# One plan for all eight PSUM banks, attention scores in rounds of 256 columns, another order in the first norm, and a fourth home for q, k and v

## The chip, the cores and the metric

The kernel runs on one core of a Trainium2 chip. The time is that of the device in microseconds (us), the median of several executions. Lower is better. TensorE is called PE here, VectorE DVE, ScalarE ACT, GpSimd POOL and SyncE SP; PEld is the loading of weights into the PE array.

## What is computed

The input `x` has 2048 rows of 512 in bf16. Four layers are applied to it, attention A, feed-forward B, A, B, each on a normalised `x` and added back to it:

```
x = x + A(layernorm(x));  x = x + B(layernorm(x));  x = x + A(layernorm(x));  x = x + B(layernorm(x))

A: 32 heads of 16, the 2048 rows in 4 segments of 512
   logits = q_s k_s^T * 16**-0.5, causal inside the segment;  a_dot = softmax(logits) v_s
   a_mem  = phi(q_s) M / (phi(q_s) z + 1e-6);   o = g a_mem + (1-g) a_dot
   M += phi(k_s)^T v_s;  z += sum phi(k_s);     phi(t) = t+1 if t > 0 else exp(t);   result o wo
B: gelu(x w_gate) * (x w_up) w_down, 512 -> 1792 -> 512
```

## The kernel before

**Work.** The rows are handled as 8 passes `k` (4 segments in each of the two attention layers), every pass with an `Att(k)` and an `Ffn(k)`. Weights stay in SBUF. A dense product is one PSUM bank (128 partitions x 512 columns of fp32): 4 matmuls of 512 columns for q, k, v, wo, gate and up, 14 for down. In a pass these are 4 blocks each of q and k, 4 row tiles of v, 4 of wo, 14 tiles of gate, 14 of up and 4 row tiles of down.

**Scores.** Heads come in 4 blocks `b` and 2 parities `par`, four heads at a time, each head in its own 32 rows of the PE array (row tiles; line 794). With odd heads `kB`, a copy of `kf` with the even heads masked out, takes the place of `kf`. Causal scores of one head against 512 queries are four pieces of 512, 384, 256 and 128 columns, by key tile `ki`. Five steps (`PAIRS`) of four heads x 512 columns serve two parities, so a pass has 20 steps. A step fills four banks `st`, in two halves of two heads; ACT takes the exponential of each half (line 828, 128x1024), POOL zeroes what lies above the diagonal (line 817). When the planner finds only the first half's banks free, it issues the step as two separate halves (`score_now`, `score`). When a parity is complete, a "flush" multiplies `pt` with `vaug` (v with a column for the sum) in column tiles of 32 into a dense bank (line 847), and DVE divides and transposes it back (lines 859 to 874).

**Modes of PE.** A matmul uses the whole 128x128 array (line 370, `whole`), four column tiles of 32 (line 367, `columns`, used for dense products near a flush) or four row tiles (`rows`, scores). The planner keeps `ck.mode` and charges 0.097 us for a change of it.

**The order of work** is written out by a planner inside the kernel: the engines run in manual order, and `order()` keeps clocks of PE, ACT, DVE, POOL and SP and issues an instruction when its clock says that it is due. Dense products, memory products and flushes are `Item`s with a due time; free PSUM banks and `pt` buffers are counted in `banks`, `st_free` and `step_free`; numbers in `POLICY` shift the due times. Where nothing is ready while scores are still to come, a product of ones (`warm`) fills the gap. The order on each engine is therefore fixed in the program: a late operand stalls the whole engine.

**Banks.** Four banks (`M_BANKS`, tiles `m0` to `m3`) belong to dense products and flushes, four to scores (`st0` and `st1`, two banks each).

**The start.** Tiles of `x` for the first segment arrive by four DMAs, two issued by SP and two by ACT (line 248), the gate vector `beta` behind them on ACT's queue, and then SP issues wk, wq, the second segment of x, wv and the third segment of x (line 239). PE runs 16 `warm` products. The norm of the first segment is written by hand: DVE computes the statistics of tiles 0 to 2 (lines 1044, 1047), ACT those of tile 3 (lines 1061, 1062, stored in `shift` and `mv`) behind two small exponentials of `beta` (lines 300, 302); a small DVE addition (line 1050) and POOL's power (line 1054) give the scales of tiles 0 and 1 and then of 2 and 3; then DVE writes the four normalised tiles (line 426), PE transposes them (line 468) and the first k and q follow (lines 744, 749).

**The end.** In the second layer the row tiles of down are added to `x` by DVE (line 914) and written out by SP (line 239) one by one.

Of the kernel before, what the change touches and what calls it, by code (L numbers as in the profile page):

```python
# [34 lines left out]
WARM = 16  # L35
PAIRS = 5
STEPS = 4 * PAIRS
BY_PE = {("xnTf", 0), ("xnTf", 1), ("xnTf", NK - 1)}
M_BANKS = 4
PT_STEPS = 5  # L40
# [5 lines left out]
SPLIT = 8  # L46
# [4 lines left out]
    flush_wait=5.276, piece_slack=1.333, kb_slack=3.5, mem_slack=1.0, margin=1.079, qk_due=0.75, e_q=0.099,  # L51
    e_k=0.898, exp_slack=-1.27, e_slack=2.265, phi_slack=3.273, gelu_slack=-1.15, act_evict=0.538,
    first_evict=0.928, gate_step=0.002, up_due=1.3, up_step=0.02, down_due=1.6, down_step=0.042, upd_due=0.5,
    v0_due=-0.54, x1_at=11.9, x2_at=22.0, cut_slack=0.0, direct=1, gelu_tiles=3, kb_dve=1, phi_pool=2,
    half_steps=1)
# [54 lines left out]
class Clocks:  # L110
# [6 lines left out]
    def __init__(self):  # L117
        self.pe = 0.0
        self.mode = "whole"
        self.act, self.dve, self.pool, self.sp = Engine(0.09), Engine(0.07), Engine(), Engine()  # L120
        self.engines = (self.dve, self.act, self.pool, self.sp)
        self.later, self.seq, self.waiting = [], 0, []
        self.dma = 0.0
        self.ev = {}
# [47 lines left out]
    def has(self, *names, by=None):  # L172
        t = self.pe if by is None else by
        return all(self.ev.get(n, 1e9) <= t for n in names)
# [24 lines left out]
class Item:  # L199


    def __init__(self, due, ready, ops, done, kind, ps):
        self.due, self.ready, self.ops, self.done, self.kind, self.ps = due, ready, ops, done, kind, ps
        self.posted = 0.0
# [17 lines left out]
def order(pol, nc, cst, seg, wrk, psp, st_pool, A_x, A_wq, A_wk, A_wv, A_wo, A_beta, B_x, B_w_gate, B_w_up, B_w_down, out):  # L222

    ck = Clocks()
    ev = ck.ev
    xf = A_x.flatten_outer_dims()
# [8 lines left out]
    wd_sb = cst.tile([P, FT, D], BF16, name="wd_sb")  # L235
    beta_bc = cst.tile([P, H], BF16, name="beta_bc")
# [21 lines left out]
    for n, (sb, w) in enumerate(((wg_sb, B_w_gate), (wu_sb, B_w_up))):  # L258
        for kt in range(KT):
            for h in range(2):  # L260
                c = slice(FF * h // 2, FF * (h + 1) // 2)
                pieces.append((37.0 + 1.6 * (8 * n + 2 * kt + h), 224, lambda sb=sb, w=w, kt=kt, c=c: load(
                    sb[:, kt, c], w_view(w)[:, kt, c])))
    for h in range(7):
        r = slice(2 * h, 2 * h + 2)
        pieces.append((94.0 + 2.0 * h, 256, lambda r=r: load(
# [7 lines left out]
    def bank_tile(i, shape, dtype=F32):  # L274
        return psp.tile(shape, dtype, tag=f"m{i}", bufs=1, name="m")

    def keep_warm(n, bank):
        if n:
            ps = bank_tile(bank, [P, L])
        for _ in range(n):  # L280
            nc.tensor.matmul(ps[:], lhsT=warm[:], rhs=wide, start=True, stop=True)
# [18 lines left out]
    nc.scalar.activation(out=tmp_e[:], in_=beta_bc[:], func=ACT.Exp)  # L300
    tmp_e2 = cst.tile([P, H], F32, name="tmp_e2")
    nc.scalar.activation(out=tmp_e2[:], in_=beta_bc[:], func=ACT.Exp, scale=-1.0)
# [3 lines left out]
    vaugs = [cst.tile([P, TPS, VW + 15], BF16, name=f"vaug{i}") for i in range(SETS)]  # L306
# [10 lines left out]
    def later_constants():  # L317
# [4 lines left out]
        for n, va in enumerate(vaugs):  # L322
            ck.dve.post(13.0 + 3.0 * n, NORMAL, (0.4, lambda va=va: column(va), None))
# [10 lines left out]
    banks = [0.0] * M_BANKS  # L334

    class Psum:
        def __init__(self, shape=(P, L), dtype=F32):
            self.shape, self.dtype, self.bank, self.t = list(shape), dtype, None, None

        def __call__(self):  # L340
            if self.t is None:
                self.t = bank_tile(self.bank, self.shape, self.dtype)
            return self.t
# [4 lines left out]
    def evict(ps, dst, src, told, slack=NORMAL):  # L348
# [7 lines left out]
        first = pol.first_evict if ("scores", pol.half_steps - 1) not in ev and pol.half_steps else pol.act_evict  # L356
# [26 lines left out]
    class Norm:  # L383
# [80 lines left out]
        def first_turn(self, j):  # L464
            xn = self.first_xn[j]
            ps = bank_tile((j + 1) % M_BANKS, [P, KT, P], BF16)
# [3 lines left out]
            if j < 2:  # L470
                nc.scalar.activation(out=dst, in_=ps[:], func=ACT.Copy)
            else:
                nc.vector.tensor_copy(out=dst, in_=ps[:])
# [7 lines left out]
    class Att:  # L481
        def __init__(self, k):
            self.k, self.s, self.tt0 = k, k % NSEG, TPS * (k % NSEG)
            self.norm = Norm(("xnTa", k), self.tt0, f"xnTa{k % 2}", NORMAL, lambda: k < 2 or ("qkv", k - 2) in ev)
            self.vaug = vaugs[k % SETS]
# [8 lines left out]
        def add_items(self):  # L494
            k, s = self.k, self.s

            def storage():
                return k < SETS or (("scores", k - SETS) in ev and self.phi_done(k - SETS))
# [8 lines left out]
            def qk(b, w, done):  # L507
                ps = Psum()
                pairs = [(lambda kt=kt: w[:, kt, b * P:(b + 1) * P], lambda kt=kt: self.norm.xnT[:, kt, :])
                         for kt in range(KT)]  # L510
                return Item(k - pol.qk_due + 0.01 * b, lambda: storage() and ck.has(("xnTa", k)), dense(ps, pairs),
                            lambda: (made(), self.counted(), done(b, ps)), kind="qk", ps=ps)
# [30 lines left out]
            def v(j):  # L543
# [4 lines left out]
                def done():  # L548
# [6 lines left out]
                            lambda: ck.has(("xnTa", k)) and (k < SETS or ("flush", k - SETS, 3, 1) in ev),  # L555
                            dense(ps, pairs), done, kind="v", ps=ps)
# [61 lines left out]
        def mem_items(self):  # L618
# [5 lines left out]
            den = Psum((P, TPS, 4, 8))  # L624

            def den_mm(j, b):
                nc.tensor.matmul(den()[:, j, b, :], lhsT=self.phiq[:, b, j * P:(j + 1) * P],
                                 rhs=mem_state[k - 1][1][:, b, :], start=True, stop=True)

            def den_done():  # L630
                def add():
# [3 lines left out]
                        out=self.rdm[:], in0=den()[:], scalar=EPS_MEM, op0=ALU.add, op1=ALU.mult,  # L635
# [8 lines left out]
                              den_done, kind="mem", ps=den))  # L644

            def num(b):
# [32 lines left out]
                def go():  # L679
# [5 lines left out]
                            kind="mem", ps=ps)  # L685
# [4 lines left out]
        def upd_item(self):  # L690
            k = self.k
            psm = Psum((P, 4, P))
# [6 lines left out]
            def m(c):  # L699
                j, b = divmod(c, 4)  # L700
                nc.tensor.matmul(psm()[:, b, :], lhsT=self.phik[:, j, b * P:(b + 1) * P],  # L701
                                 rhs=by_head(self.vaug)[:, j, 8 * b:8 * b + 8, 0:DH], start=(c == 0), stop=(c == n_mm - 1))

            def done():
# [7 lines left out]
                def gated(src):  # L712
                    return lambda: nc.vector.tensor_tensor(out=made[0][:], in0=src()[:],
# [10 lines left out]
                if self.s == 0:  # L724
                    steps = [(0.154, lambda: nc.vector.tensor_copy(out=zacc[:], in_=self.zk[:]), kept),
                             (0.683, gated(psm), None),
                             (0.2, z, told),
                             (0.683, lambda: nc.vector.tensor_copy(out=macc[:], in_=psm()[:]), psm.read)]
                else:
                    steps = [(0.683, lambda: nc.vector.tensor_tensor(out=macc[:], in0=macc[:], in1=psm()[:],  # L730
# [3 lines left out]
                             (0.683, gated(lambda: macc), None),  # L734
# [4 lines left out]
                              done, kind="upd", ps=psm))  # L739
# [13 lines left out]
        def score_ready(self, t):  # L753
            b, i = divmod(t, PAIRS)
            if self.k == t == 0:
                return ck.has(("q", 0, 0), by=ck.pe - 0.055)
            names = [("q", self.k, b), ("k", self.k, b)] + ([("kB", self.k, b)] if i > 1 else [])
            return ck.has(*names, by=ck.pe - 0.055)

        def scores(self, t, halves):  # L760
            k = self.k
            b, i = divmod(t, PAIRS)
            if halves[0] == 0:
                if i == 0:
                    self.pts = {}
                if i in (0, 3):
                    self.masked = self.masked[-2 if k < SPLIT else -1:] if i else []
                self.pt = wrk.tile([P, 4, L], BF16, tag="pt", bufs=PT_STEPS, name="pt")
                self.step_from = step_free.pop(0)
            masked, pt = self.masked, self.pt  # L770
            parts = [
                [(0, 0, 0)],
                [(0, 1, 0), (0, 3, 3 * P)],
                [(0, 2, 0), (1, 2, 2 * P)],
                [(1, 0, 0)],
                [(1, 1, 0), (1, 3, 3 * P)],
            ][i]

            split = k < SPLIT
            if not split and not whole_st:  # L780
                whole_st.append(st_pool("stw"))
            if split:
                sts = {n: psp_st.tile([P, 2, L], F32, tag=f"st{n}", bufs=1, name="st") for n in halves}
            else:
                st = whole_st[0].tile([P, 4, L], F32, tag="st", bufs=1, name="st")
            for par, ki, c0 in parts:
                N = L - P * ki
                for j in [2 * n + m for n in halves for m in range(2)]:
# [4 lines left out]
                    dst = sts[j // 2][:, j % 2, c0:c0 + N] if split else st[:, j, c0:c0 + N]  # L793
                    nc.tensor.matmul(dst, lhsT=lhsT[rows, b, P * ki:P * ki + P],  # L794
                                     rhs=self.q[rows, b, P * ki:L], start=True, stop=True, tile_position=(32 * j, 0))
                self.pts[par, ki] = (pt, c0)
            ck.tiling("rows")
            begun = ck.pe
            ck.on_pe(0.23)
            for first, width, src in [(2 * n, 2, sts[n]) for n in halves] if split else [(0, 4, st)]:  # L800
                part = pt[:, first:first + width, :]
                blocks = part.rearrange("p j (a c) -> p j a c", c=P)
                if i == 2:
                    flat = part.rearrange("p j (a c) -> p (j a) c", c=P)
                    diag = [(flat[:, 8 * n:8 * n + 8:2, :], 4) for n in range(width // 2)]
                elif len(parts) == 1:
                    diag = [(blocks[:, :, 0, :], width)]
                else:
                    diag = [(blocks[:, :, 0, :], width), (blocks[:, :, 3, :], width)]
                done = []  # L810
                masked.append(done)
# [461 lines left out]
```

## Time and profile before

| | |
|---|---|
| median of 3 runs | 558.58 us (558.19 to 558.64) |
| span of the profiled execution | 557.3 us, 1.3 us under the median |
| PE busy | 550.3 us (99%) |
| DVE, ACT, POOL busy | 459.8, 440.7, 325.0 us (83, 79, 58%) |
| exponentials of scores, ACT | 310.0 us, 320 of 1.02 us |
| masks, POOL | 205.3 us in 448 instructions |
| granted PE clock | 1.00 |

The span is the time from the first to the last instruction of one execution; the difference to the median lies around it. Busy times of matmuls are modelled ends of a pipeline: a matmul of 512 columns has a row of 0.38 us, but the next one starts 0.216 us later. Start to start is therefore what a matmul costs, and a busy PE can still hold gaps. "Idle before" is the time that an engine stood still ahead of an instruction, with the instruction that released it.

### The profile page before, as it was taken

To read this page: it belongs to the slowest core of one execution; us is meant where nothing else is said; L and a number is where in the kernel's file an instruction comes from. 1 tells how busy PE (TensorE), PEld (TensorE's weight loads), DVE (VectorE), ACT (ScalarE), POOL (GpSimd) and SP (SyncE) were. 2 spreads that over 40 slices of the span, in tenths; PEclk is the share of its full clock that TensorE was granted. 3 is DMA by queue.
4 is the path that set the end of the run, shared out by engine and by line. 5 is a ranking of instruction groups with operands and counts; after the bars stand their busy time and mean duration, and the time that the engine had idled before them with its cause. 6 is when DMAs were issued, how large, how long until landed. Compare 5 with 4: busy or idle time off the path is not lost.

```text
span 557.3 us, 18772 instructions
## 1 busy us (share of the span) xinstructions
PE 550.3 (99%) x8114; PEld 248.9 (45%) x8114; DVE 459.8 (83%) x852; ACT 440.7 (79%) x510; POOL 325.0 (58%) x554
## 2 busy tenths in 40 slices
PE   8999999999999999999999999999999999999997
PEld 3434454444444444444444444444444444445443
DVE  4979999989988899878978998888887996878061
ACT  4899999998899778988789878988789777770600
POOL 2599866568754959447757877666855745310000
PEclk9999999999999999999999999999999999999999
DMA  7248503600140016110400024100421003200001
GB/s 226 41 99 242 107 13 53 149 13 3 30 78 11 12 21 86 32 12 3 68 11 2 9 42 78 30 3 12 69 62 19 1 12 68 39 2 31 9 2 38
DMA packets 64339, 25.60 MB, mean 46 GB/s; under 512 B 54272, under 2 KB 64256, under 8 KB 64256
## 3 DMA queue, kind: packets, MB, share of 16 engines
q1 hardware_dynamic: 63824, 24.13, 21.3%
q8 instruction: 63, 1.03, 0.8%
q10 hardware_dynamic: 432, 0.27, 0.2%
q14 instruction: 20, 0.16, 0.1%
HBM read 9.71 MB, written 2.10 MB: 21 GB/s over the span
## 4 chain that ended last, share of the span: by engine, by line
PE 89%; DVE 5%; ACT 2%; DMA 1%; POOL 1%; issue 1%; ACTq 0%; DVEq 0%
PE m L367 48%; PE m L370 22%; PE st L794 9%; PE m L847 6%; PE m L701 1%; ACT pt L828 1%; PE m L650 1%; DMA beta_bc<-in_A_beta_dram 1%; DVE byq L859 1%; DVE aT L874 1%; DVE xn L426 1%; DMA xnT<-xn 1%; POOL pt L817 1%; DVE st L396 1%; PE m L456 0%
## 5 line engine op out<-in xcount | busy, mean ns | idle before, releaser
L828 ACT ACTIVATE pt<-st 128x1024 bf16<-128x1024 f32 x320 | 310.0, 1024 | 56.3 <-PE st L794 50.2
L817 POOL TENSOR_SCALAR_AFFINE_SELECT pt<-pt 128x256 bf16<-128x256 bf16 (+1 forms) x448 | 205.3, 480 | 144.5 <-ACT pt L828 138.9
L976 DVE TENSOR_TENSOR gel<-gel,m 128x512 bf16<-128x512 bf16 x112 | 75.9, 684 | 30.2 <-PE m L370 16.8
L367 PE MATMUL m<-wd_sb,gel 128*32 128x512 bf16 x1304 | 77.7, 380 | 0.0
L367 PE MATMUL m<-xnT,wu_sb 128*32 128x512 bf16 x1212 | 71.8, 380 | 0.2 <-DVE gel L976 0.2
L914 DVE TENSOR_TENSOR x_sb<-x_sb,m 128x512 bf16<-128x512 bf16 x64 | 42.3, 673 | 20.4 <-PE m L370 11.8
L367 PE MATMUL m<-xnT,wg_sb 128*32 128x512 bf16 x912 | 56.8, 380 | 0.3 <-DVE am L660 0.3
L602 POOL TENSOR_SCALAR e<-e 128x512 bf16<-128x512 bf16 x36 | 54.9, 1529 | 2.3 <-ACT e L584 0.6
L527 POOL TENSOR_SCALAR kB<-kf,maskB 128x512 bf16<-128x512 bf16 x28 | 44.7, 1595 | 16.6 <-DVE kf L357 16.4
L370 PE MATMUL m<-xnT,wg_sb 128*128 128x512 bf16 x220 | 51.6, 379 | 0.1
L859 DVE STREAM_TRANSPOSE byq<-m 128x512 f32<-128x512 f32 x64 | 45.0, 705 | 6.5 <-PE m L847 6.3
L367 PEld LDWEIGHTS <-gel 128*32 128x32 bf16 x1304 | 32.6, 97 | 33.0 <-issue 4.4
L847 PE MATMUL m<-pt,vaug 128*32 128x512 bf16 (+3 forms) x1024 | 46.3, 300 | 0.0
L357 DVE CAST gel<-m 128x512 bf16<-128x512 f32 x59 | 39.3, 681 | 7.8 <-PE m L367 7.1
L367 PEld LDWEIGHTS <-wu_sb 128*32 128x32 bf16 x1212 | 31.0, 97 | 31.1 <-issue 3.5
L1021 ACT ACTIVATE gel<-gel 128x1536 bf16<-128x1536 bf16 (+1 forms) x35 | 43.3, 1302 | 0.1
L396 DVE BATCH_NORM_STATS2 st<-x_sb 128x6 f32<-128x512 bf16 x60 | 40.4, 673 | 0.2
L794 PE MATMUL st<-q,kf 16*128 16x384 bf16 (+3 forms) x512 | 39.5, 302 | 0.2
L794 PE MATMUL st<-q,kB 32*128 32x128 bf16 (+3 forms) x512 | 37.3, 300 | 0.0
L847 PEld LDWEIGHTS <-vaug 128*32 128x32 bf16 x1024 | 25.6, 97 | 22.6 <-issue 3.4
L367 PEld LDWEIGHTS <-wg_sb 128*32 128x32 bf16 x912 | 22.3, 96 | 23.7 <-issue 7.1
L370 PE MATMUL m<-xnT,wu_sb 128*128 128x512 bf16 x145 | 32.8, 379 | 0.0
(118 smaller groups left out, 723.0 us busy)
## 6 DMA issues: line engine op xcount, KB each, us to landing
out_dram<-x_sb SPq DMA_DIRECT2D x16, 128.0 KB, 1.7
wg_sb<-in_B_w_gate_dram SPq DMA_DIRECT2D x8, 224.0 KB, 4.5
wu_sb<-in_B_w_up_dram SPq DMA_DIRECT2D x8, 224.0 KB, 5.3
wd_sb<-in_B_w_down_dram SPq DMA_DIRECT2D x7, 256.0 KB, 3.3
x_sb<-in_A_x_dram SPq DMA_DIRECT2D x3, 512.0 KB, 6.4
xnT<-xn SPq DMA_TRANSPOSE x48, 2.5
wv_sb<-in_A_wv_dram SPq DMA_DIRECT2D x1, 512.0 KB, 7.1
wo_sb<-in_A_wo_dram SPq DMA_DIRECT2D x4, 128.0 KB, 2.3
```

The lines of the kernel that those rows point to most:

```text
L367: nc.tensor.matmul(out[r], lhsT=lhsT[:, r], rhs=rhs, start=start, stop=stop, tile_position=(0, 32 * c))
L370: nc.tensor.matmul(out, lhsT=lhsT, rhs=rhs, start=start, stop=stop)
L396: nc.vector.bn_stats(out=self.st6[:, 0, :], in_=x_sb[:, self.tt0 + j, :])
L527: job.post(t, pol.kb_slack if k else NORMAL, (cost, lambda: eng.tensor_scalar(out=self.kB[:, b, :], in0=self.kf[:, b, :], scalar1=maskB[:, ...
L602: return lambda: eng.tensor_scalar(out=e[0][:], in0=e[0][:], scalar1=1.0, scalar2=None, op0=ALU.min)
L794: nc.tensor.matmul(dst, lhsT=lhsT[rows, b, P * ki:P * ki + P], rhs=self.q[rows, b, P * ki:L], start=True, stop=True, tile_position=(32 * j ...
L817: nc.gpsimd.affine_select(out=dv, in_=dv, pattern=[[0, w], [1, P]], compare_op=ALU.is_ge, fill=0.0, base=0, channel_multiplier=-1)
L828: 0.18 + 0.422 * width, lambda src=src, part=part: nc.scalar.activation(out=part, in_=src[:], func=ACT.Exp, scale=SCALE), told), table="exp")
L847: nc.tensor.matmul(ps()[32 * j:32 * j + 32, P * ki:L], lhsT=self.vaug[:, ki, h * (DH + 1):h * (DH + 1) + 32], rhs=two[:, j, c0:c0 + L - P ...
L859: nc.vector.transpose(out=self.byq[:, par, :, :].rearrange("p a c -> p (a c)"), in_=ps()[:])
L976: ck.dve.post(ck.made(), NORMAL, (0.683, lambda: nc.vector.tensor_tensor(out=g, in0=g, in1=ps()[:], op=ALU.mult), lambda t: (ps.read(t), e ...
L1021: return (0.205 + 0.427 * (f1 - f0), lambda: nc.scalar.activation(out=g, in_=g, func=ACT.Gelu_apprx_tanh), lambda t: self.gelu_done(t, f0, ...
```

## The change

- `ps_all` is one PSUM tile of eight banks. Scores take pairs of banks, dense products and flushes single banks, all from the same list `banks`. `pick` gives a dense product the other half of a pair that is in use already, else a new one while fewer than `cap=4` pairs are held by dense work.
- Scores come in rounds of four heads x 256 columns (`PIECES`), 5 for each parity, 40 a pass. With the policy's `rounds=2` always two rounds are issued together (as many columns as a step before), into two pairs of banks; there are no halves any more. Each pair has one exponential of 128x1024 as before; one mask instruction covers a pair, without the round that has no diagonal (`NO_DIAG`). The flush has six pieces for each head instead of four. `pt` is one tile of ten slots, each a pair's result.
- From the second pass on, a pair of rounds is issued only when ACT's backlog of exponentials is below `starve=0.518`.
- q, kf and kB of pass 0 lie in `wd_sb` and its `vaug` in `gel_sb`, so that passes 1 to 3 have the three other sets; w_down is loaded once pass 0 has done with them.
- The first norm: ACT computes tile 3's statistics before the exponentials of `beta`, tiles 0 and 1 are normalised before `shift` is used; 15 `warm` products instead of 16, and the one between the transposes goes.
- The last row tile of down in each pass of the second layer is made, added and written out in two halves of 256 columns.
- The planner's numbers: a new `POLICY`; for instance kB of pass 0 is made on POOL (`kb_dve=0`), the cut of phi on POOL from pass 1 on (`phi_pool=1`), and v of pass 0 has the due time -1.527 instead of -0.54.

```diff
-WARM = 16
-PAIRS = 5
-STEPS = 4 * PAIRS
+WARM = 15
+UNIT = 256
+ROUNDS = 5
+STEPS = 8 * ROUNDS
+PIECES = [[(0, 0, 256, 0)], [(0, 256, 256, 0)], [(1, 128, 256, 0)], [(3, 384, 128, 0), (1, 384, 128, 128)],
+          [(2, 256, 256, 0)]]
...
-    upd_due=0.5,
-    v0_due=-0.54, x1_at=11.9, x2_at=22.0, cut_slack=0.0, direct=1, gelu_tiles=3, kb_dve=1, phi_pool=2,
-    half_steps=1)
+    upd_due=-0.151, v0_due=-1.527, x1_at=10.541, x2_at=16.065, x3_at=40.015, cut_slack=6.049, direct=1,
+    gelu_tiles=3, kb_dve=0, phi_pool=1, rounds=2, early=1, starve=0.518, cap=4, fuse=1)
...
+    ps_all = psp.tile([P, BANKS, L], F32, tag="ps", bufs=1, name="ps")
+    ps_pairs = ps_all[:].rearrange("p (a b) c -> p a (b c)", b=2)
+    pt_all = wrk.tile([P, PT_SLOTS, 4, UNIT], BF16, tag="pt", bufs=1, name="pt")
...
-                self.q, self.kf, self.kB = (seg.tile([P, KT, L], BF16, tag=f"{n}{k % SETS}", bufs=1, name=n)
-                                            for n in ("q", "kf", "kB"))
+                if k:
+                    self.q, self.kf, self.kB = (seg.tile([P, KT, L], BF16, tag=f"{n}{k % SETS}", bufs=1, name=n)
+                                                for n in ("q", "kf", "kB"))
+                else:
+                    self.q, self.kf, self.kB = (wd_sb[:, KT * i:KT * (i + 1), :] for i in range(3))
...
+    def pick():
+
+        got = [i for i in range(BANKS) if free(i, ck.pe)]
+        mine = len({i // 2 for i in range(BANKS) if banks[i] > ck.pe and i // 2 not in score_pairs})
+        half = [i for i in got if not free(i ^ 1, ck.pe)]
         if half:
-            return (1,) if free[1] else ()
-        if all(free):
-            return (0, 1)
-        other = any(not j[4] and j[0] <= st_free[1] for j in ck.act.jobs)
-        return (0,) if k < SPLIT and free[0] and (idle or k < pol.half_steps and not other) else ()
+            return min(half, key=lambda i: (-banks[i ^ 1], banks[i]))
+        if got and (mine < pol.cap or not streams):
+            return max(got, key=lambda i: i)
+        return None
...
     nc.scalar.activation(out=spare[:, 1, :], in_=x_sb[:, TPS - 1, :], func=ACT.Square, scale=root, bias=shift[:],
                          accum_out=n0.mv[:, TPS - 1, 1:2])
+
+    nc.scalar.activation(out=tmp_e[:], in_=beta_bc[:], func=ACT.Exp)
+    nc.scalar.activation(out=tmp_e2[:], in_=beta_bc[:], func=ACT.Exp, scale=-1.0)
...
-    first_scale(1)
+    first_scale(2, 4)
+    n0.first_xn = [n0.normed(0, 0), n0.normed(1, 1)]
     nc.vector.tensor_scalar(out=n0.mv[:, TPS - 1, 0:1], in0=shift[:], scalar1=-1.0 / root, scalar2=None, op0=ALU.mult)
+    n0.first_xn += [n0.normed(2, 2), n0.normed(3, 3)]
...
-    n0.first_xn = [n0.normed(j, j) for j in range(TPS)]
     n0.first_turn(0)
     n0.first_turn(1)
-    keep_warm(1, 0)
...
+            if self.last:
+                downs[-1:] = [down(TPS - 1, 0, D // 2), down(TPS - 1, D // 2, D)]
```

More of the change, by code (lines that the diff above doesn't have):

```diff
@@ L1151, in open_item @@
         items.remove(it)
-        it.ps.bank = min((i for i in range(M_BANKS)), key=lambda i: banks[i])
-        banks[it.ps.bank] = 1e9
-        return it
-    def score(halves):
-        k, t = streams[0]
-        att[k].scores(t, halves)
-        if halves[-1]:
-            streams.pop(0)
-        got = [it for it in items if it.kind == "flush" and it.ready()]
-        if got and min(banks) <= ck.pe:
-            it = open_item(got)
+        it.ps.bank = bank
+        banks[bank] = 1e9
+        return it
```

437 lines of the change are left out of this document (234 added, 203 removed).

## The prediction

> **What bounds the kernel now.** I read the page first, for the engine that is never idle, and the chain that ended last.
>
> ```profile
> span 557.3 us, 18772 instructions
> PE 550.3 (99%) x8114; PEld 248.9 (45%) x8114; DVE 459.8 (83%) x852; ACT 440.7 (79%) x510; POOL 325.0 (58%) x554
> ...
> PE 89%; DVE 5%; ACT 2%; DMA 1%; POOL 1%; issue 1%; ACTq 0%; DVEq 0%
> ```
>
> Then the busy times by stage, to see whether that holds everywhere (columns: length, PE, PEld, DVE, ACT, POOL, clock, DMA):
>
> ```profile
> 0.00:14.00 14.00, 11.49 (x64) 5.10 (x64) 6.92 (x23) 6.97 (x14) 3.54 (x13) 1.00 0.75 225
> 14.00:70.00 56.00, 55.59 (x856) 22.74 (x856) 50.50 (x105) 52.47 (x65) 46.31 (x78) 1.00 0.52 122
> 70.00:490.00 420.00, 419.20 (x6576) 190.66 (x6568) 368.67 (x671) 362.73 (x409) 271.50 (x456) 1.00 0.19 35
> ```
>
> After the first 14 us PE has no holes, ACT has 14% free and POOL more. So the time is what PE's own program costs, plus a start and an end. A busy PE can hide losses, so next comes the timeline of PE, by starts.
>
> ```profile
> 13.70 0.39 PE L794 MATMUL st<-q,kf 16*128 16x384 bf16 x4
> 14.02 0.39 PE L370 MATMUL m<-xnT,wk_sb 128*128 128x512 bf16 x1
> ...
> 149.76 0.50 PE L847 MATMUL m<-pt,vaug 128*32 128x256 bf16 x12
> 150.19 0.40 PE L794 MATMUL st<-q,kf 16*128 16x384 bf16 x8
> 150.52 1.04 PE L370 MATMUL m<-xnT,wg_sb 128*128 128x512 bf16 x4
> 151.40 0.61 PE L650 MATMUL m<-mblk,phiq 128*128 128x128 bf16 x8
> 151.84 1.03 PE L370 MATMUL m<-xnT,wg_sb 128*128 128x512 bf16 x4
> 152.80 0.29 PE L794 MATMUL st<-q,kf 16*128 16x256 bf16 x4
> ```
>
> Three prices stand in it. A 512-column matmul costs 0.216: the four at 150.52 take until 151.40. A change of mode costs 0.10: four matmuls from 151.84 would end at 152.70, and the scores start at 152.80; on the way out, 150.19 to 150.52 is 0.33 for 512 columns of four heads, again 0.11 too much. And a score step cut in halves pays twice: 13.70 to 14.02 is 0.32 for two heads, as long as four heads take at 150.19.
>
> Last the timeline of the start.
>
> ```profile
> 4.88 1.15 SPq L239 DMA_DIRECT2D wv_sb<-in_A_wv_dram  x1
> 5.77 0.18 DVE L1047 BATCH_NORM_AGGREGATE mv<-st 128x2 f32<-128x6 f32 x1
> 5.86 0.23 ACT L300 ACTIVATE tmp_e<-beta_bc 128x32 f32<-128x32 bf16 x1 [2.38 <-DMA beta_bc<-in_A_beta_dram]
> 6.11 0.61 ACT L1061 ACTIVATE spare<-x_sb 128x512 bf16<-128x512 bf16 x1
> 6.85 0.72 ACT L1062 ACTIVATE spare<-x_sb,shift 128x512 bf16<-128x512 bf16 x1
> 7.70 0.17 DVE L1050 TENSOR_SCALAR mv<-mv 128x2 f32<-128x2 f32 x1 [1.75 <-ACT spare L1062]
> 7.84 0.73 DVE L426 TENSOR_SCALAR xn<-x_sb,mv,rs 128x512 bf16<-128x512 bf16 x2
> 8.30 0.72 PE L468 MATMUL m<-ident,xn 128*128 128x128 bf16 x8 [1.34 <-DVE xn L426]
> 8.83 0.73 DVE L426 TENSOR_SCALAR xn<-x_sb,mv,rs 128x512 bf16<-128x512 bf16 x2 [0.27 <-POOL rs L1054]
> 11.75 0.40 PE L794 MATMUL st<-q,kf 16*128 16x512 bf16 x4
> ```
>
> ACT stands for 2.4 us until `beta` lands, with tile 3 of x, landed at 4.3, behind it; DVE, POOL and PE follow ACT.
>
> **The change part by part.** The order of instructions in both programs gives the counts; durations are from the profiled execution, whose span of 557.3 lies 1.3 under the median 558.58. The sum is made on the span, and 1.3 is added.
>
> *Streaming.* From the first score on, PE streams 483.7 us of columns in both programs: scores 34.1, flushes 34.1, warm 8.1, the rest 407.4. Nothing is gained or lost; neither is filler.
>
> *Modes.* PE changes mode 351 times after the first score, before 380. 29 x 0.10 = -2.9.
>
> *Halves.* Before, 160 score steps are 178 runs: 18 are cut, and each then takes 2 x 0.213 instead of 0.213. Now all 160 groups are whole. 18 x 0.213 = -3.8.
>
> *More, smaller matmuls.* There are 1,122 more after the first score (512 each in scores and flushes). The row is the flush at 149.76: 12 matmuls, 768 columns, 0.43 to the next start, of which 0.32 is columns and 0.10 the mode; about 0.01 for three quads. Two more quads in 64 flushes and one or two in 128 score pieces, at 3 to 4 ns each, and the split downs: +1.0. The Trainium skill's "TensorEngine Tiling (Array Packing)", section Instruction Overhead, states about 60 cycles for each matmul; added to each that would be an estimated 1,122 x 25 ns = 28 us at the page's 2.4 GHz. Read as a least length, as the page's own example has it, it is nothing for 128 columns; the flush row agrees with this second reading.
>
> *Two short pieces in a row* (128 columns) in 64 score runs: the trace has none in row tiles. Lower end 0: whole-array 128s with a weight load each follow at 0.056 (eight at 151.40, 0.61 with the last one's tail of 0.22). Upper end: each of 128 waits out a weight load of 92 ns instead of 53, 5.0 us. I take 0, the chained row being nearest.
>
> *The start.* With tile 3 first, ACT starts at 4.3 and needs 0.74 and 0.85, as from 6.11 to 7.70: 5.9. DVE's addition waits for the aggregate until 5.95 anyhow, so it ends at 6.15; the first xn then lets PE transpose 0.46 later, at 6.6 instead of 8.30 (15 warm products end at 6.74). POOL's second power starts at 6.2, takes 0.85, and xn 2 comes at 7.1 instead of 8.83: -1.75 to the first score, which moves from 11.75 to 10.0. The exponentials of `beta` lie behind ACT's two, ahead of its transposed copies at 7.0, and are hidden there; wk and wq land by 6.6 for their first columns.
>
> *But what follows the first score is now v*, not q, and v needs wv. SP's queue is unchanged in this place: wv is issued at 4.88 and lands 7.1 later, at 12.0. The first v product is in PE's order 0.32 behind the first score, at 10.3, and waits 1.7. All of PE stands behind it. Before, 0.32 behind the first score was 12.07. So the start as a whole gives only -0.1. A bound from both sides: -1.75 if v did not wait, +0.1 if the landing slips by 0.2.
>
> *Pass 1's first q.* DVE has the eviction of the first v ahead of the statistics of segment 1, so this chain waits as well. By rows from 13.0 on (0.67 evictions, 0.66 and 0.18 statistics, 0.55 constants, two more evictions) xn of pass 1 starts at about 21.2 instead of 19.57; the four transposing DMAs then took 8 us to the last landing: about 29. PE asks for it at 26.9 + 1.7 = 28.6. Before, PE waited 0.5 there. Between 0 and +1.5 more; I take +0.8.
>
> *ACT, DVE, POOL.* ACT gets 25 evictions more at 0.61 and two table loads fewer at 1.28: +12.6. DVE loses about as many at 0.68, four kB and eight cuts. POOL gains 8 x 1.53 and 4 x 1.60 for these, +18.6, and loses about 24 by wider masks (0.66 for four blocks, 0.43 for two). All of it is costed at nothing: PE's stream covers it, with ACT at 363 of 420 us rising by some 11. If that cover is gone, exponentials come late, then masks, flushes and PE.
>
> *pt slots, w_down, the fourth set.* Ten slots hold what five buffers held. w_down is issued about 95 to 107 as before, and the first down product comes at about 116: 0, covered by the gate and up products.
>
> *The end.* After PE's last matmul come an addition and a store: a 256-column copy out of PSUM took 0.42 (line 1094), the addition 0.69: -0.3. The store 0 to -0.3; I take 0.
>
> Sum: -2.9 - 3.8 + 1.0 - 0.1 + 0.8 - 0.3 = -5.3. Span 552.0, time **553.3**.
>
> **The rivals.**
> *B, v does not wait long* (the landing comes earlier or the first score later): up to -1.7, time 551.6. For: PE's start is the earlier one only by my chain. Against: the queue is the same.
> *C, part of the gain is given back at the shared banks.* A score group now needs two whole free pairs, and a dense product may sit in one of them until DVE (0.68) or ACT (0.61) has emptied it. 0.02 us on each of 160 groups is +3.2: 556.5.
> *D, slower: the same mechanism at full size.* At 0.1 us a group it is +16: 569.3. It erases the gain from 5.3/160 = 0.033 us a group, and is slower by 0.2% from 0.04. For: ACT gets the extra evictions. Against: before, dense matmuls waited for DVE 0.5 us in all, and now eight banks rather than four can take them.
> *E, PE's clock falls in the wait for wv.* Before, an idle 1.34 left it at 1.00; 1.7 is a little more. At half speed for some 3.4 us it costs 1.7 to 3.4: about 555.8. The Trainium skill's "TensorE: Matmul & The Clock Gate", section Why this matters for your kernels, warns of gaps over about 3 us; this gap would be shorter.
> *F, smaller matmuls are dear.* At 22 ns each, what the 8-column products cost beyond their columns, 1,122 make +25: 577, slower. The flush row speaks against it, and the skill's 60 cycles, added to each matmul, would do this too.
>
> **How the numbers follow.** Forecast 0.60, B 0.08, C 0.12, D 0.13, E 0.05, F 0.02. C reaches from 554 to 560, some 0.05 of it inside 0.2% of no change (1.1 us, about what a measurement of this kernel can tell). Faster 0.60 + 0.08 + 0.05 + 0.07 = 0.80, same 0.05, slower 0.15. Own range of the forecast: 551.3 to 555.5. The range 550.5 to 559 leaves out D and F and about 0.05 below and in C.
>
> **What would show it.** Modes and halves: score runs of 8 and 12 matmuls only, each 0.33 long to the next start. Start: transposes at 6.7, first scores at 10.0, a wait of PE for the DMA of wv of 1.7 to about 12.0, then a wait for the transposed xn near 29. Columns: 12-matmul runs over 0.36 would show the short pieces. Banks: waits of the score line or of dense matmuls for DVE or ACT beyond 1 us in all would point to C or D, as would gaps in PE from 70 to 490 us. The clock row shows E.

## The result, and the profile after

The changed kernel takes 561.8 us (median; 561.76 to 562.32) against 558.4 for the kernel before on the same chip, a ratio of 1.0058 (95% interval 1.0045 to 1.0070). The forecast was 553.3: the change makes the kernel slower by 0.6% instead of faster by 0.9%.

The page of the changed kernel, its span, its engines and the chain that ended last by engine:

```profile
span 560.1 us, 21158 instructions
...
PE 542.6 (97%) x9193; PEld 271.0 (48%) x9234; DVE 449.8 (80%) x821; ACT 450.9 (81%) x533; POOL 323.8 (58%) x438
...
PE 69%; DVE 20%; DMA 4%; issue 3%; ACT 2%; POOL 1%; SPq 0%; ACTq 0%; DVEq 0%
```

DVE has less work than before (449.8 against 459.8 us), yet its share of the chain goes from 5 to 20%: PE now waits for it. (PE's busy time looks lower than it is: 41 matmuls of 512 columns have no record in this trace, as the counts of PE and PEld tell.) The busy times by stage, columns as before:

```profile
0.00:14.00 14.00, 10.04 (x61) 4.76 (x62) 6.11 (x21) 7.24 (x14) 5.38 (x15) 1.00 0.73 225
14.00:70.00 56.00, 54.54 (x1063) 25.69 (x1068) 52.08 (x106) 52.30 (x65) 50.18 (x65) 1.00 0.53 125
70.00:490.00 420.00, 411.25 (x7426) 204.78 (x7456) 358.14 (x640) 376.59 (x434) 266.94 (x357) 1.00 0.18 34
```

ACT has 13.9 us more work in the 420 us of the middle (forecast: some 11), and is still idle for 10% of it. So no engine has become the bound as a whole; the waits are single ones. The seven largest waits of PE from 14 us on (who waited, for whom: us in total, times, longest); the first line, nine gaps as long as one matmul, fits the missing records, and the kernel before, which lacks none, has no such line:

```profile
PE ps L379 <- issue: 1.4, 9, 0.2
PE ps L793 <- ACT pt L1199: 1.3, 2, 0.7
PE ps L642 <- DVE phiq L600: 1.1, 1, 1.1
PE ps L793 <- DVE byq L824: 0.8, 2, 0.6
PE ps L376 <- DVE wd_sb L366: 0.6, 1, 0.6
PE ps L376 <- ACT pt L1199: 0.6, 2, 0.4
PE ps L793 <- DVE am L675: 0.6, 1, 0.6
```

In the kernel before, the same view from 70 to 490 us has two lines, of 0.3 and 0.2 us. Two of these waits in the timeline (start, length, engine, line):

```profile
151.81 0.28 PE L793 MATMUL ps<-q,kf 16*128 16x256 bf16 x2
151.93 0.68 DVE L675 TENSOR_TENSOR am<-ps,rdm 128x512 bf16<-128x512 f32 x1
...
152.66 0.40 PE L793 MATMUL ps<-q,kf 16*128 16x256 bf16 x10 [0.57 <-DVE am L675]
...
153.12 1.02 ACT L1199 ACTIVATE pt<-ps 128x1024 bf16<-128x1024 f32 x1 [1.48 <-PE ps L793]
```

```profile
217.52 0.63 ACT L596 ACTIVATE e<-kf 128x512 bf16<-128x512 bf16 x1 [1.78 <-DMA phik<-e]
218.06 1.92 ACT L1199 ACTIVATE pt<-ps 128x1024 bf16<-128x1024 f32 x2
...
219.11 0.28 PE L793 MATMUL ps<-q,kf 16*128 16x256 bf16 x2 [0.68 <-ACT pt L1199]
```

At 151.8 a score group has begun in one pair of banks, and its second piece needs a bank that DVE is still emptying of a memory product (line 675). All of PE stands, and ACT, whose next exponential comes out of this group, stands 1.5 us. At 217.5 ACT itself stood 1.8 us for a late transfer, the exponentials behind it came late, and PE waited twice at banks that they were to empty.

To add up the waits I set the start of every matmul in the trace against the sum of the prices of all matmuls ahead of it (those of the prediction: 0.213 for 512 columns, 4 ns for a group of four side by side, 0.10 a change of mode), and listed each jump over 0.25 us, called a single wait here. Before, there are five from 14 us on, 1.6 us in all. In the changed kernel there are sixteen, 9.8 us: 7.5 at a bank that its reader had not yet emptied (one more wait than the expectations below count), 2.0 for late data, 0.3 at the end. The wait for wv at the start, 2.1, comes on top. The balance up to the start of the last matmul, 553.6 us before and 556.7 after:

| us | before | after | |
|---|---|---|---|
| PE's own program (columns, modes, halves, small matmuls), as priced | 541.6 | 535.6 | -6.0 |
| single waits from 14 us on | 1.6 | 9.8 | +8.2 |
| the rest: start with wv, small gaps | 10.4 | 11.3 | +0.9 |

So the gain was there, and the waits took it and more.

### The profile page after: what moved, and what is told of

Read it like the earlier page. It is cut to its first block, busy times and chain, and to the rows that moved or that the text cites. A ratio compares the mean times of both kernels' runs of the same rounds, so it can differ in the third digit from the quotient of the medians.

```text
span 560.1 us, 21158 instructions
## 1 busy us (share of the span) xinstructions
PE 542.6 (97%) x9193; PEld 271.0 (48%) x9234; DVE 449.8 (80%) x821; ACT 450.9 (81%) x533; POOL 323.8 (58%) x438
## 4 chain that ended last, share of the span: by engine, by line
PE 69%; DVE 20%; DMA 4%; issue 3%; ACT 2%; POOL 1%; SPq 0%; ACTq 0%; DVEq 0%
PE ps L376 37%; PE ps L379 19%; PE ps L793 6%; PE ps L809 4%; DVE st L405 3%; DVE xn L435 3%; DVE x_sb L879 2%; DVE byq L824 2%; DMA phik<-e 2%; ACT pt L1199 2%; DVE gel_sb L366 1%; DVE ab L832 1%; DMA wv_sb<-in_A_wv_dram 1%; DVE phiq L600 1%; PE ps L665 1%
## 5 line engine op out<-in xcount | busy, mean ns | idle before, releaser
L1199 ACT ACTIVATE pt<-ps 128x1024 bf16<-128x1024 f32 x320 | 309.7, 1026 | 36.3 <-PE ps L793 32.4
L1205 POOL TENSOR_SCALAR_AFFINE_SELECT pt<-pt 128x512 bf16<-128x512 bf16 (+1 forms) x320 | 184.1, 589 | 132.5 <-ACT pt L1199 131.7
L939 DVE TENSOR_TENSOR gel_sb<-gel_sb,ps 128x512 bf16<-128x512 bf16 x112 | 74.5, 683 | 28.4 <-PE ps L379 17.1
L376 PE MATMUL ps<-wd_sb,gel_sb 128*32 128x512 bf16 (+1 forms) x1296 | 75.2, 370 | 0.0
L879 DVE TENSOR_TENSOR x_sb<-x_sb,ps 128x512 bf16<-128x512 bf16 (+1 forms) x68 | 43.2, 645 | 30.9 <-PE ps L376 17.0
L376 PE MATMUL ps<-xnT,wg_sb 128*32 128x512 bf16 x1056 | 64.4, 380 | 0.6 <-DVE gel_sb L366 0.4
L376 PE MATMUL ps<-xnT,wu_sb 128*32 128x512 bf16 x1128 | 64.8, 379 | 0.0
L824 DVE STREAM_TRANSPOSE byq<-ps 128x512 f32<-128x512 f32 x64 | 45.1, 706 | 13.4 <-PE ps L809 12.9
L991 ACT ACTIVATE gel_sb<-gel_sb 128x1536 bf16<-128x1536 bf16 (+1 forms) x35 | 43.4, 1304 | 0.1
L379 PE MATMUL ps<-xnT,wg_sb 128*128 128x512 bf16 x170 | 41.9, 379 | 1.1 <-issue 0.5
```

The source lines that it names most:

```text
L376: nc.tensor.matmul(out[r], lhsT=lhsT[:, r], rhs=rhs, start=start, stop=stop, tile_position=(0, 32 * c))
L379: nc.tensor.matmul(out, lhsT=lhsT, rhs=rhs, start=start, stop=stop)
L824: nc.vector.transpose(out=self.byq[:, par, :, :].rearrange("p a c -> p (a c)"), in_=ps()[:])
L879: ck.dve.post(ck.made(), slack, (0.15 + 0.00104 * (c1 - c0), lambda: nc.vector.tensor_tensor(out=xt, in0=xt, in1=ps()[:, 0:c1 - c0], op=AL ...
L939: ck.dve.post(ck.made(), NORMAL, (0.683, lambda: nc.vector.tensor_tensor(out=g, in0=g, in1=ps()[:], op=ALU.mult), lambda t: (ps.read(t), e ...
L1199: nc.scalar.activation(out=pt_all[:, s0:s1 + 1:max(s1 - s0, 1), :, :].rearrange("p s u c -> p s (u c)"), in_=ps_pairs[:, p0:p1 + 1:max(p1 ...
```

## The experiments

### The start

**wv ahead of the second segment of x**, with the plan unchanged:

```diff
+    load(w_att["v"][:], w_view(A_wv))
     load_x(1)
-    load(w_att["v"][:], w_view(A_wv))
```

> The changed kernel, with wv issued ahead of the second segment of x; the plan and every order on PE, ACT, DVE and POOL stay. Theory 1 (the wait for wv at the first v product, 2.1 us in the trace, lies on the path): about 2 us faster than the changed kernel, 559.8. Rival (PE's later waits would have swallowed it): the same as the changed kernel, 561.8 within 0.3. Also possible: the second segment of x, then last, comes too late for its statistics at 13 us and gives part of it back.

Measured: 560.0 us, ratio 1.0026 (1.0014 to 1.0037). The timelines of PE in the changed kernel and in this one:

```profile
10.09 0.40 PE L793 MATMUL ps<-wd_sb 16*128 16x256 bf16 x8
12.49 0.81 PE L379 MATMUL ps<-wv_sb,xnT 128*128 128x512 bf16 x2 [2.00 <-DMA wv_sb<-in_A_wv_dram]
```

```profile
10.06 0.40 PE L793 MATMUL ps<-wd_sb 16*128 16x256 bf16 x8
10.39 1.69 PE L379 MATMUL ps<-wv_sb,xnT 128*128 128x512 bf16 x6
12.01 0.40 PE L793 MATMUL ps<-wd_sb 16*128 16x256 bf16 x12
```

The wait is gone and 1.8 us with it. The rest of the loss stays, with most single waits from 14 us on at the same places. (They come to 11.2 us here, but the profiled execution took 562.3 us, 2.3 more than the median, with PE's clock at 0.50 for 3.4 us from 219.6 us on. So this sum is not that of a typical execution.)

**The old first norm in the changed kernel** (ACT's two exponentials of `beta` first, four `xn` in a row, 16 `warm` products and one between the transposes):

```diff
-WARM = 15
+WARM = 16
...
-    n0.first_xn = [n0.normed(0, 0), n0.normed(1, 1)]
...
-    n0.first_xn += [n0.normed(2, 2), n0.normed(3, 3)]
+    n0.first_xn = [n0.normed(j, j) for j in range(TPS)]
...
+    keep_warm(1, 0)
```

> The changed kernel with the first norm in its old order (exponentials of beta ahead, 16 warm products, one between the transposes); the plan behind it stays. Theory 1 (the new order gains 1.75 us up to the first score, all of it lost again in the wait for wv): no difference, 561.8 within 0.3, the first score near 11.75 and no wait for wv. Rival (the new order is worth its 1.75 us): 563.5.

Measured: 561.3 us, 1.0048 (1.0036 to 1.0061), 0.5 under the changed kernel where at most 0.3 was expected. The first scores start at 11.56, and PE does not wait for wv. In this kernel the new norm is worth nothing: what it gains, PE waits for wv.

**The new first norm in the kernel before** (the same edit the other way round):

> The kernel before with the first norm in the new order alone (ACT's statistics ahead of the exponentials of beta, tiles 0 and 1 normalised first, 15 warm products, none between the transposes). Theory 1: behind the first score stands q, not v, so nothing waits for wv: 1.7 us faster than before, 556.7. Rival (another load, wq or x, becomes the wait): 558.4 within 0.3.

Measured: 556.8 us, 0.9968 (0.9956 to 0.9980). That is 1.8 us under the kernel before in the same series (558.6), as expected: it has q behind the first score, not v, and keeps the whole gain.

### How soon a bank is used again

**The kernel before, with the bank that came free last in place of the one free for longest.** Order and plan are unchanged, only the numbers of dense banks differ (the same rule goes for the products of ones):

```diff
-        it.ps.bank = min((i for i in range(M_BANKS)), key=lambda i: banks[i])
+        it.ps.bank = max((i for i in range(M_BANKS) if banks[i] <= ck.pe), key=lambda i: banks[i])
...
```

> The kernel before with one thing changed: of the free dense banks the planner takes the one freed last and not the one freed first. Its plan, every order and the planned end stay; only bank numbers differ, and the share of dense products whose bank was planned free less than 0.3 us earlier rises from 6 to 26% (the changed kernel has 20%). Theory 2 (the changed kernel is slower since its banks are reused so soon that a late eviction stops PE): slower by 4 to 7 us, 562 to 565, with waits of PE for DVE of 0.3 to 0.9 us each. Rival (the waits come from the other engines' load, not from how soon a bank is reused): 558.4 within 0.5.

Measured: 562.1 us, 1.0064 (1.0051 to 1.0077): as slow as the changed kernel, and 3.5 us over the kernel before in the same series, just under the 4 to 7 expected. Its waits of PE have three lines that the kernel before has not, the longest for ACT and not for DVE, and its chain has DVE at 10%, from 5:

```profile
PE m L370 <- ACT gel L941: 1.1, 1, 1.1
PE m L370 <- DVE ab L867: 0.5, 1, 0.5
PE m L370 <- DVE x_sb L914: 0.4, 1, 0.4
```

Set side by side weight load by weight load, this trace falls behind that of the kernel before by 3.0 us from 14 us on, in steps of up to 1.3 us; 1.6 of it come after 490 us. So by the planner's clocks every bank is free in time, and on the chip it is not: a reader ends off its clock, by tenths of a us and once by 1.1, and with the bank free for longest PE rarely notices.

**A margin for readers.** The next kernels add a margin to the clock at which a read sets a bank free. The planned end is the planner's PE clock at the end of the program; time less planned end is what the chip takes beyond it. With 0.2 us alone, settings unchanged, the plan ends 10.5 us later; for the others the planner's settings (`POLICY`) were searched again, by random moves that kept the plan with the earliest end on the planner's own clocks, and wv is loaded first.

```diff
-            banks[self.bank] = t + 0.05
+            banks[self.bank] = t + 0.05 + pol.rest
```

> The changed kernel with the load of wv ahead of x's second half, with 0.3 us added to the planner's clock at which a read sets a bank free, and with the planner's settings searched again, so that its planned end stays where it was (543.3 us against 542.8). Theory 1, that products and scores lose their time waiting at banks whose reader ends a few tenths of a us later than planned: of the 13 such waits (7.5 us in the changed kernel) those up to 0.3 us disappear and the others shrink by 0.3 each (3.9 us), so the time ends 543.3 + 19.0 (the changed kernel's time less its planned end) - 1.8 (wv, measured) - 3.9 to 7.5 = 553.0 to 556.6 us, below the kernel before. Rival: the distance of the chip from the plan has nothing to do with when banks come free (it is the price of mode switches, small matmuls or data waits): 543.3 + 19.0 - 1.8 = 560.5 us.

> The same with 0.2 us in place of 0.3, from another search (planned end 543.9 us). Theory 1: each of the 13 waits shrinks by 0.2 at least, 2.6 us, to 5 us in all: 543.9 + 17.2 - 2.6 to 5 = 556.1 to 558.5 us, more than with 0.3. Rival: 543.9 + 17.2 = 561.1 us.

> A second plan with a margin of 0.3 us, from another search (planned end 543.7 us). Theory 1: the time less the planned end is again near 10.8 (9.5 to 13.5): 553 to 557 us. Rival (the first was a lucky plan): like without a margin, 15 or more: 558.7 us or later.

> A margin of 0.45 us (planned end 546.6 us: the searches found no earlier one). Theory 1: the distance falls further, to 7 to 10 us (the kernel before, whose planned end is 552.5, has 5.9, or 4.2 with the new first norm): 553.6 to 556.6 us, and the gain from 0.3 to 0.45 is about what the plan loses. Rival (the distance has nothing to do with the margin): 546.6 + 10.8 = 557.4 us or later.

> The changed kernel with one number changed: 0.2 us added to the clock at which a read sets a bank free, settings as they are (planned end 553.3 us, 10.5 later, since these settings were not found for it). Theory 2: the time less the planned end falls from 19.0 to 13.5 to 15.5, since single waits at banks fall from 7.5 us to 2 to 4: 566.8 to 568.8 us. Rival (the waits have nothing to do with the margin): 553.3 + 19.0 = 572.3 us.

Measured: 554.1 us with 0.3 (ratio 0.9916, 0.9903 to 0.9929), 558.4 with 0.2 (0.9987, 0.9975 to 1.0000), 554.1 with the second 0.3 (0.9915, 0.9902 to 0.9928), 555.9 with 0.45 (0.9947, 0.9931 to 0.9962), and 565.6 with 0.2 alone (1.0130, 1.0115 to 1.0145). The last one is the plainest: one number changed, and the distance of time and plan falls from 19.0 to 12.3 us, further than the 13.5 to 15.5 expected, while the plan itself has become 10.5 longer. But its single waits fall by 3.3 us only (table below); what the other 3.4 are, in a plan so much longer, is not shown. What PE waits for from 14 us on in the second plan with 0.3:

```profile
PE ps L377 <- ACT gel_sb L368: 0.6, 1, 0.6
PE ps L810 <- POOL pt L1206: 0.4, 1, 0.4
PE ps L794 <- ACT pt L1200: 0.4, 1, 0.4
PE ps L377 <- DVE q L367: 0.3, 1, 0.3
PE ps L380 <- DVE q L367: 0.3, 1, 0.3
PE ps L466 <- DVE x_sb L880: 0.2, 1, 0.2
```

By these five alone my theory would have stood: banks are used again too soon, a margin mends it. It needed a control.

### The same search without a margin

wv first, the settings searched as long, margin 0, three times:

> The control of the two before: wv ahead of x's second half and the planner's settings searched as long, without a margin (planned end 542.2 us, the earliest of all). So far the time less the planned end is 17.2 us without a margin, 14.5 with 0.2, 10.8 with 0.3. Theory 1 (it is the margin that counts): 542.2 + 15 to 18.5 = 557 to 560.5 us, later than the plan that promises to end 1.1 us later. Rival (the search found better settings, and the margin is by the way): 542.2 + 10.8 = 553 us.

> The control again: wv ahead, no margin, settings from another search (planned end 542.5 us; they lie nearer to those of the changed kernel). The control without a margin took 554.3 us, time less planned end 12.2, where the changed kernel's own settings have 17.2. Theory 2 (without a margin the waits at banks fall as they happen to, and differ by us from plan to plan; the changed kernel's plan is a bad draw): between 12 and 17.2, so 554.5 to 559.7 us, and not the same as the other control. Theory 1 as it stood (every plan without a margin has some 17): 559.5. Rival (any longer search finds what the first control found): 554.7.

> A third control without a margin (planned end 542.6 us). Theory 2: between 12 and 17.2 above the plan, so 554.6 to 559.8 us. Theory 1: 559.6. Rival: 554.8.

Measured: 554.3 us (0.9921, 0.9908 to 0.9934), 555.1 (0.9942, 0.9928 to 0.9956) and 553.5 (0.9915, 0.9901 to 0.9928). All three are faster than both kernels. The first expectation missed by 2.7 us, the last lies below its range too, and the rival's number was near each time (within 1.3 us): the margin isn't what makes these kernels fast. The five largest waits of PE from 14 us on in the third, to set beside those of the changed kernel:

```profile
PE ps L377 <- DVE wd_sb L367: 0.8, 1, 0.8
PE ps L380 <- DVE byq L825: 0.4, 1, 0.4
PE ps L377 <- ACT pt L1200: 0.4, 1, 0.4
PE ps L810 <- DVE x_sb L880: 0.3, 1, 0.3
PE ps L810 <- POOL pt L1206: 0.2, 1, 0.2
```

By the planner's clocks, 249 of 1053 uses of a bank between 20 and 480 us come less than 0.3 us after it was freed in the changed kernel (a score group counts for each of its four banks), and 260, 256 and 263 in these three. By this count the risk is the same; what came of it is not.

**Neighbours of the changed kernel's settings**, wv first, no margin, one setting moved a little in each:

```diff
-phi_slack=4.283
+phi_slack=4.854
```

(for the second, `down_step` from 0.058 to 0.054; for the third, `starve` from 0.518 to 0.5)

> The changed kernel with wv ahead and one setting moved a little (phi_slack 4.283 to 4.854): the order on PE is the same up to 14% of the program and another one after it; planned end 543.3 us. Theory 2 (the waits are a draw of each plan, and the changed kernel's is a bad one): the time less the planned end lies where the three controls have it, 11 to 13, or between these and 17.2: 554.3 to 558.5 us. Rival (the changed kernel's settings, not the draw, make the waits): 17.2 again, 560.5 us.

> The same with down_step 0.058 to 0.054: the order differs from 35% of the program on; planned end 542.8 us. Of the 9 us of single waits behind 20 us, some 6 lie behind this point, among them all behind 200 us. Theory 2: 2 to 4 of them go: 556 to 558 us. Rival: 560.0 us.

> The same with starve 0.518 to 0.500: the order differs from 66% of the program on, so all waits up to some 365 us are kept, and only some 1.3 us behind that can go; planned end 542.5 us. Both theories: 558.4 to 559.7 us, and the same single waits as in the run with wv ahead up to there.

Measured: 557.6 us (0.9981, 0.9970 to 0.9991), 557.2 (0.9972, 0.9964 to 0.9981) and 559.2 (1.0009, 1.0001 to 1.0018): each in its expected range. Against wv first (560.0) the two that part early gain 2.4 and 2.8 us, the late one 0.8. The third has the changed kernel's waits up to the point where it parts (those near 207, 218 and 296 us among them), the second has its own from 35% on. All plans together, sorted by the last column but one:

| kernel | margin | planned end | time | time less plan | single waits from 14 us |
|---|---|---|---|---|---|
| changed | 0 | 542.8 | 561.8 | 19.0 | 9.8, and 2.1 for wv |
| wv first | 0 | 542.8 | 560.0 | 17.2 | 11.2, in an execution of 562.3 |
| neighbour, late | 0 | 542.5 | 559.2 | 16.6 | 8.8 |
| searched | 0.2 | 543.9 | 558.4 | 14.5 | 8.1, in an execution of 559.6; 3.1 of it one late transfer, and a slower clock behind that |
| neighbour, middle | 0 | 542.8 | 557.2 | 14.4 | 7.6 |
| neighbour, early | 0 | 543.3 | 557.6 | 14.3 | 7.1 |
| searched, second | 0 | 542.5 | 555.1 | 12.6 | 5.5 |
| 0.2 alone | 0.2 | 553.3 | 565.6 | 12.3 | 6.5, and 2.3 for wv |
| searched, first | 0 | 542.2 | 554.3 | 12.2 | 6.7 |
| searched, third | 0 | 542.6 | 553.5 | 10.9 | 3.8 |
| searched | 0.3 | 543.3 | 554.1 | 10.8 | 4.7 |
| searched, again | 0.3 | 543.7 | 554.1 | 10.4 | 4.1 |
| searched | 0.45 | 546.6 | 555.9 | 9.3 | 4.2 |

The last column is of one execution each, which lies up to 2.3 us off the median. A kernel's time is its plan plus what its order happens to wait, and a rest that hardly varies. Without a margin the single waits come to 3.8 to 9.8 us in seven orders of nearly one planned end (wv first has the changed kernel's order); the changed kernel holds the worst. I call that a draw, but this is argued, not shown. The seven are not independent: the neighbours share the changed kernel's order on PE up to where they part, and the three searched plans its first 10, 31 and 25%. And all three searched plans lie nearer to their planned end than the changed kernel and its neighbours, so that something in the settings makes the waits is not excluded. With 0.3 or more the single waits lie at 4 to 5, and the plan pays for that with what it might have saved.

### The kernel before, searched as long

With the new first norm, its banks as they were; then also with wv first:

> The kernel before with the new first norm and with its own settings searched again for as long (planned end 549.8 us against 552.5). Its reuse of banks stays as it was, the bank that has been free longest first, with scores in banks of their own. Time less planned end was 4.2 us with the new norm alone: if that holds for a new plan, 554.0 us, and the shared banks would be worth nothing over it. Rival (a tighter plan loses here too): 556 us or more.

> The retuned kernel before with the load of wv ahead of x's second segment: its new settings put v behind the first score as the changed kernel's do, and PE waited 2.5 us for wv there. Theory (that wait and the slower clock behind it are all that kept it from 554.0): 554.0 to 555.9 us (549.8 planned plus 4.2, or 558.4 less 2.5), so that the shared banks are worth 0 to 2.5 us over it by the controls at 553.5 to 555.1. Rival (the tighter plan loses elsewhere): 557 us or more.

Measured: 558.4 us (0.9995, 0.9981 to 1.0010) and 556.5 (0.9960, 0.9947 to 0.9974). The first waited 2.5 us for wv, because its new settings also put v behind the first score (this is the profiled execution, 562.0 us, 3.7 over the median); the second still waits 1.0 there, the three searched ones 0.3 to 0.7. So 2.7 us less of planned end became 0.3 less of time over the 556.8 of the new norm alone. The second number lies between the two expected. Over it, the changed kernel with settings searched as long (553.5 to 555.1) is 1.4 to 3.0 us faster. That is one plan against three, and the worth of all that is left of the change: shared banks, rounds, the fourth home and the halved last tile; no run takes these apart. The second lies 6.7 us over its planned end, less than any plan with shared banks (9.3 to 19.0).

## Why the prediction was wrong

- **Modes, halves, more matmuls** (-5.7): held as a sum, as far as prices can tell. So priced, PE's own program falls by 6.0, and what is left beside the single waits is 8.8 to 10.4 us in the ten plans with wv first, without the one with the late transfer. Score runs of 8 and 12 matmuls take 0.33 to the next start in the changed kernel, so short pieces cost nothing, and smaller matmuls aren't dear (F). The 2.4 GHz in the prediction's estimate of 28 us is a figure of the Trainium skill's "TensorE: Matmul & The Clock Gate", section What's actually happening, and not of the page named beside it; the trace agrees with it, at 0.216 us for 512 columns.
- **The start** (-0.1): transposes at 6.67, first scores at 10.09, as forecast; PE waited 2.1 for wv instead of 1.7, so the gain of 1.7 is not just eaten but some 0.4 lost: what follows the first scores starts at 12.49, before at 12.08. The three runs on the start show the parts: norm -1.8, wv 1.8.
- **Pass 1's first q** (+0.8 near 29 us): not seen there. The planner put products of ones ahead of it, and one of these waited 0.8 at 25.0 for DVE's eviction.
- **The end** (-0.3): from the start of the last matmul to the end of the span 3.7 us became 3.4.
- **The clock** (E): 1.00 in the profiled execution, right for this gap.
- **"ACT, DVE, POOL. All of it is costed at nothing: PE's stream covers it"** is the step that failed: 8.2 us more of single waits, in place of 0. The sums of busy time were roughly right and beside the point. The sign that the prediction named for C or D, over 1 us of waits at banks, came with 7.5. What I held against D was that eight banks rather than four can take a dense product, and that dense matmuls had waited 0.5 us before. Both are true of a rule that takes the bank free for longest; the new `pick` takes one because its neighbour is in use, and a score group takes any two free pairs. By the planner's clocks, uses less than 0.3 us after the freeing rise from 6 to 20% of the dense ones. For scores they fall: 156 of 308 uses of a pair `st` before, 26% of the uses of a bank after. Yet before, where only ACT's exponentials empty the score banks, PE's waits have no line for ACT at all. So closeness alone is not the price. New is whom a score group can wait for: 38 of its 620 uses of a bank come that soon behind the reader of a dense product, before none could. The rule of `pick` stood in the diff, and D's own bound named the point: slower from 0.04 us a group. The waits at banks became 7.5/160 = 0.047, though not all stood at score groups. D had 0.13.
- What neither forecast nor D had: how much this depends on the order. The same rule gives 553.5 us in another order with wv moved; that it lies next to the forecast is luck, since the forecast had neither these settings nor any waits at banks. What makes one order wait more than its neighbour stays open beyond the single cases shown: the number of close uses doesn't tell it.

## What to carry to other kernels

Where the order of every engine is written out, a plan that fills its engines tighter ends earlier on paper and waits more on the chip: price a change of such a plan by whom each engine can be made to wait for, and how soon after the plan's own clock, not by busy shares alone. Test a change of the planner on several plans before judging it, with a control that has been searched as long, since here one plan or another made up to 6.5 us of difference and the change itself 1.4 to 3 over the one retuned plan of the kernel before. And when work moves to the front, move its load with it.

## What the runs showed of the hardware

PE's clock fell after shorter gaps than I had thought. In the changed kernel 2.0 us of idle PE at the start left it at 1.00; with 0.2 alone 2.2 us did not. Busy times by stretch of the changed kernel, and then of that one (the clock is the third number from the end):

```profile
12.49:14.50 2.01, 1.96 (x19) 0.89 (x20) 0.88 (x2) 0.03 (x1) 0.61 (x2) 1.00 0.11 39
14.50:17.00 2.50, 2.50 (x15) 1.01 (x19) 2.35 (x8) 2.47 (x4) 1.10 (x2) 1.00 0.00 0
```

```profile
12.83:14.50 1.67, 1.67 (x6) 0.72 (x6) 0.31 (x1) 0.00 (x0) 0.43 (x2) 0.70 0.15 52
14.50:16.00 1.50, 1.50 (x16) 0.43 (x14) 1.47 (x4) 0.05 (x1) 0.00 (x0) 0.50 0.00 0
```

After 2.5 us of idle PE in the retuned kernel before, the clock stood at 0.50 from 14.2 to 21.0 us, and after the 3.1 us for a late transfer in the searched plan with 0.2, at 0.50 from 408.2 to 411.6. With wv first it fell behind two shorter gaps with 0.3 us of scores between them, and stood at 0.50 from 219.6 to 223.0:

```profile
217.79 0.28 PE L793 MATMUL ps<-q,kf 16*128 16x256 bf16 x2 [1.11 <-ACT pt L1199]
218.70 0.28 PE L793 MATMUL ps<-q,kf 16*128 16x256 bf16 x2 [0.63 <-ACT pt L1199]
```

```profile
217.00:220.00 3.00, 1.58 (x24) 0.54 (x23) 2.93 (x7) 3.00 (x5) 2.83 (x4) 0.93 0.43 87
220.00:225.00 5.00, 5.00 (x35) 2.40 (x32) 3.86 (x7) 3.26 (x6) 2.36 (x4) 0.70 0.27 53
```

The changed kernel has gaps of 0.68 and 0.63 in the same place and stays at 1.00. Each of these stretches at 0.50 lasted 3.4 us or twice that. Nor does it come every time: of the four executions with 0.2 alone, two had a mean clock of 0.997, which is what 3.4 us at 0.50 make, and two of 1.00.

The Trainium skill's "TensorE: Matmul & The Clock Gate", section Why this matters for your kernels, asks for no gaps over about 3 us. Of these gaps only the one of 3.1 us is so long, so here the measurement decides: 2.2 us can be enough, and so can 1.1 and 0.6 close together.
